# Residuals of three groups formed in PSUM by a unit product, and earlier loads in the last group

## The chip, the cores and the metric

One core of one Trainium2 chip runs the whole program in one launch. The metric is device time in microseconds, smaller is better. The engines are named as in the profile: PE (TensorE matmuls), PEld (its weight loads), DVE (VectorE), ACT (ScalarE), POOL (GpSimd) and SP (SyncE, which issues most DMAs here). PSUM is the memory that PE writes; SBUF is the other on-chip memory. Line numbers as L424 are those of the kernel before; those of the changed kernel are said to be so.

## The reference

Three stages in a row: a delta-rule attention with state, then two token-mixing blocks. The change lies in the attention.

```
q, k, v: (4, 8, 768, 48) fp32; beta: (4, 8, 768)
k_n = k / (norm(k) + 1e-06)
for t in range(768):                     # per batch and head, state is 48 x 48
    y[t]  = q[t] @ state
    v_old = state^T k_n[t]
    state = state + beta[t] * outer(k_n[t], v[t] - v_old)
x = y as (4, 768, 384)
h = gelu(x @ w_in); u, v = halves of h; v_n = layernorm(v) * g_ln
x = x + (u * (w_sg @ v_n + b_sg)) @ w_out
xk, xr = mixes of x with x one token earlier
out = sigmoid(xr @ w_r) * (relu(xk @ w_k)**2 @ w_v)
```

## The kernel before

**The attention** goes in 12 blocks s of 64 tokens. All 32 pairs of batch and head run side by side, in two halves o = 0 and 1 of 16 pairs. Two blocks make a group (6 groups, 0 to 5). Within a block the tokens depend on each other through a triangular matrix; the solver of a group (`solver`, on DVE) inverts its 32x32 diagonal parts into a tile DT, one group ahead of its use. A half block (s, o) goes through six stages:

- `st_rq`: 16 matmuls of k with the state into a PSUM tile rk (L444) and 16 of k with q into qk (L446); then the **residual**, and ACT's copies of qk (L453), which POOL masks (L454).
- `st_d0`: the first 32 tokens solved: 16 matmuls of DT with the residual, over rk (L432); ACT copies the result to u (L461).
- `st_l`: what they add to the other 32 tokens (L468), then the residual again.
- `st_d1`: the second 32 solved (L432), copied into the SQ tile by ACT (L479).
- `st_s` updates the state (L488, ACT's L494), `st_y` forms the output (L502, ACT's L507) and stores it.

The residual is the sum of the scaled v and what the matmuls left in rk: one DVE instruction that reads v from SBUF and rk from PSUM and writes the tile r to SBUF (`residual`, L424, 48 times). v is scaled by POOL (`scale_v`, L417) after its load (L247, two halves of a tile vk; L248 loads k beside it), some stages ahead of the block.

The two halves run three stages apart, one stage of one half after one of the other: (0,0) rq, d0, l, d1, (0,1) rq, (0,0) s, (0,1) d0 and so on. `run` goes through these 144 stages, counted by `point[0]`; a group is 24 of them. Between stages it fills PE's list with other work: `gram` (products of k for the solver two groups ahead), units of the next block (x @ w_in: L567, L618), and, where there is none, `keep_warm` matmuls on a zero tile (L659). `background` adds to DVE's list: layernorm steps, the solver, and **jobs**. A job rounds one tile of a weight into a high and a low part (`narrow`: load L148, six DVE steps L157 to L167, POOL L168 and L111, ACT L108), and for some weights stores the two parts back (L196).

What sets the order: PE, ACT, DVE and POOL run the attention in the order in which the program writes it (a manual schedule); each engine's queue is in order, so an instruction that waits holds up those behind it. SP's queue, and DVE, ACT and POOL after the attention, are ordered by the framework's scheduler.

When a job may start is set by three numbers: one runs at a time in the stages (`RUN[1]`), started at every fifth stage of a group, and its first step may come two stages after its load was issued (`LJ`):

```python
            if jobs and len(running) < RUN[1] and n % EVERY == 0:
                start_job()
```

**The mixing stage** (`mix`, `project`, L884, L139) and the **last stage** (L986 to L1008) follow; both are dense matmuls of PE on 384 columns, with DVE and ACT splitting their operands, and in the mixing stage the rest of the jobs.

Of the kernel before, what the change touches and what calls it, by code (L numbers as in the profile page):

```python
# [7 lines left out]
F32 = mybir.dt.float32  # L8
# [3 lines left out]
AF = mybir.ActivationFunctionType  # L12
ALU = mybir.AluOpType
# [3 lines left out]
B, H, S, D = 4, 8, 768, 48  # L17
# [3 lines left out]
P = 128  # L21
# [5 lines left out]
CW = 256  # L27
NPRE = 1.2
LJ = 2
LJ0 = 7  # L30
SV = 60
B0 = 1.4
PRE = 0.8
GRAM0 = 17
SOLVE0 = 3
RUN = (3, 1)
EVERY = 5
JLAG = 1
BUDGET = (1.2, 1.6, 1.2, 1.6, 1.6, 1.6)
UNITS = (4.64, 3.48, 2.32, 4.35, 3.19, 2.32)  # L40
# [34 lines left out]
def fused_kernel(  # L75
# [18 lines left out]
    V, A, G, T = nc.vector, nc.scalar, nc.gpsimd, nc.tensor  # L94
# [46 lines left out]

    def narrow(dram, i, j, hi, lo, cw=CW, pool=stg, lag=JLAG, parts=None):

        w = CW if pool is stg else cw
        raw = pool.tile([P, 2 * w], U32, name="raw", bufs=NRAW if pool is stg else 2)
        nc.sync.dma_start(out=raw[:, :2 * cw], in_=dram[i * P:(i + 1) * P, j:j + cw].bitcast(U32))  # L148
        w_lo = vw(raw, 0, [(2, cw)])
        w_hi = vw(raw, 1, [(2, cw)])  # L150
        yield 0
        a = pool.tile([P, w], U32, name="na", bufs=NNA if pool is stg else 2)[:, :cw]
        f = w_hi.bitcast(F32)
        af = a.bitcast(F32)
        t1 = cw / 1920 + 0.16
        t2 = cw / 960 + 0.16
        V.tensor_scalar(a, w_hi, 0x7FFFFFFF, None, op0=ALU.bitwise_and)  # L157
        yield t1
        V.tensor_scalar(af, af, E_LO_F, E_HI_F, op0=ALU.max, op1=ALU.min)
        yield t1  # L160
        V.tensor_scalar(a, a, 3, 0x3FFFFFFF, op0=ALU.logical_shift_left, op1=ALU.bitwise_and)
        yield t1
        V.scalar_tensor_tensor(a, w_hi, 0xC0000000, a, op0=ALU.bitwise_and, op1=ALU.bitwise_or)
        yield t2
        V.tensor_scalar(w_hi, a, 0xFF800000, None, op0=ALU.bitwise_and)
        yield t1
        V.scalar_tensor_tensor(f, w_lo, 2.0 ** -52, f, op0=ALU.mult, op1=ALU.mult)  # L167
        G.tensor_tensor(af, f, af, op=ALU.add)  # L168
        yield t2
        if hi is None:  # L170
            hi, lo = raw[:, :cw].bitcast(F32R), af.bitcast(F32R)
            parts.extend((hi, lo))
        yield lag, lambda: split(A, G, af, hi, lo)
# [11 lines left out]
    def scratch(dram, name, nblk, n, cw=CW, pool=stg):  # L185

        hi = dp.tile([nblk, P, n], F32, name=name + "_dh")
        lo = dp.tile([nblk, P, n], F32, name=name + "_dl")

        def job(i, j):  # L190
            parts = []
            yield from narrow(dram, i, j, None, None, cw, pool, parts=parts)

            def put():
                for d, x in zip((hi, lo), parts):
                    nc.sync.dma_start(out=d[i, :, j:j + cw], in_=x.bitcast(F32))  # L196

            yield 0, put

        return hi, lo, [lambda i=i, j=j: job(i, j) for i in range(nblk) for j in range(0, n, cw)]  # L200
# [12 lines left out]
    wo_dh, wo_dl, jobs = scratch(w_out, "wo", 4, DM, DM // 2)  # L213
# [6 lines left out]
    with ExitStack() as at:  # L220
        ap1 = at.enter_context(tc.tile_pool(name="ap1", bufs=1, side="right"))
# [12 lines left out]
        kT, kt, vt = {}, {}, {}  # L234
# [15 lines left out]
        def load_q(s, o):  # L250
            for h in range(2):
                r = 64 * (1 - h)
                nc.sync.dma_start(out=SQ[o][s % 2][h][r:r + D, :, D:], in_=q_d[s, o, h])

# [6 lines left out]
        def bank():  # L261
# [5 lines left out]
        load_k(1)  # L267
        Dm = ap1.tile([P, 32, 32], F32, name="Dm")
        V.memset(Dm, 0.0)
        SQ = [[[ap1.tile([P, 8, D + C], F32, name=f"SQ{o}{i}{h}") for h in range(2)]  # L270
               for i in range(2)] for o in range(2)]
        for i in range(2):
            for o in range(2):
                E = G if i else V
                E.memset(SQ[o][i][1][32:64], 0.0)
                E.memset(SQ[o][i][0][96:128], 0.0)
                for h in range(2):
                    r = 64 * (1 - h)
                    if i == 0:
                        E.memset(SQ[o][0][h][r:r + 64, :, 0:D], 0.0)  # L280
        G.memset(xT[:, :, :, 0:1], 0.0)
# [138 lines left out]
        RQs, ysts = {}, {}  # L420

        def residual(s, o):
            t = ap2.tile([P, 8, D], F32, name="r32")
            V.tensor_tensor(t, vt[s][:, 8 * o:8 * o + 8, :], RQs[o][:, :, 0:D], op=ALU.add)  # L424
            RQs[o, "r"] = t

        def solve(s, o, q):
# [8 lines left out]
        def st_rq(s, o):  # L436
            cur, k0 = SQ[o][s % 2], 8 * o
            R = RQs[o] = ps2.tile([P, 8, D], F32, name="rk")
            Q = ps2.tile([P, 8, C], F32, name="qk")
            for p in range(8):  # L440
                for h in range(2):
                    r, b0 = 64 * (1 - h), 64 * h
                    k = kT[s][r:r + 64, k0 + p, :]
                    T.matmul(R[r:r + 64, p, :], lhsT=k, rhs=cur[h][r:r + 64, p, 0:D],  # L444
                             start=(p == 0), stop=True, skip_group_check=True)
                    T.matmul(Q[b0:b0 + 64, p, :], lhsT=k, rhs=cur[h][r:r + 64, p, D:],  # L446
                             start=(p == 0), stop=True, skip_group_check=True)
            yield
            residual(s, o)
            for h in range(2):  # L450
                b0 = 64 * h
                pt = cur[h][b0:b0 + 64, :, D:]
                A.activation(pt, Q[b0:b0 + 64], AF.Copy, scale=-1.0)  # L453
                G.affine_select(out=pt, in_=pt, pattern=[[0, 8], [1, C]],  # L454
                                compare_op=ALU.is_gt, fill=0.0, base=0, channel_multiplier=-1)
# [18 lines left out]
        def st_d1(s, o):  # L474
            solve(s, o, 32)
            yield
            for h in range(2):
                r, b0 = 64 * (1 - h), 64 * h
                A.activation(SQ[o][s % 2][h][b0:b0 + 64, :, 0:D], RQs[o][r:r + 64], AF.Copy)  # L479

# [52 lines left out]
        later, vstat, streams, point = [], {}, [], [0, 0]  # L533
# [98 lines left out]
        def fill(n):  # L632
            n += owed[0]
            while n > 0 and (units or opened[0]):
                if not opened[0]:
                    done = min([i for i, _ in running] + [n_jobs - len(jobs)])
                    ready = [u for u in units if done >= (6, 12)[u[2]]]
                    if ready:
                        units.remove(ready[0])
                        opened[0] = ready[0][1]()  # L640
                    else:
                        break
                w, f = opened[0].pop(0)
                f()
                n -= w
            owed[0] = min(n, 0)
            if n > 0 and point[0] < 144:
                idle[0] += n
                keep_warm(int(idle[0]))
                idle[0] -= int(idle[0])  # L650
# [41 lines left out]
        running = []  # L692
        jobs = in_jobs + jobs
        n_jobs = len(jobs)

        def start_job(lead=LJ):
            j = jobs.pop(0)()
            running.append((n_jobs - len(jobs) - 1, j))
            next(j)
            streams.append([point[0] + lead, j, "job"])  # L700

        def early(n, t):
            for _ in range(n):
                background(t)
                while len(running) < 2 and len(jobs) > n_rest:
                    start_job(LJ0 if point[0] else LJ)
                point[0] += 1
# [14 lines left out]
        def whole(job):  # L722
            for _, f in job:
                f()

        stages = [st_rq, st_d0, st_l, st_d1, st_s, st_y]
        rest = [lambda j=j: whole(j) for j in diag[4:]]
        k = 0
# [27 lines left out]
        def run(fn, s, o):  # L756
            g, n = divmod(point[0], 24)
            point[1] = min(g, 1) + 1
            body = fn(s, o) if point[0] else iter(())
            next(body, None)  # L760
            gg, nn = divmod(point[0] - GRAM0, 24)
            if nn == 0 and 0 <= gg and gg + 2 < NG:
                grams.extend(gram(gg + 2))
            if n == 0 and g + 1 < NG:
                streams.append([point[0] + SOLVE0, solver(g + 1), "solve"])
            if jobs and len(running) < RUN[1] and n % EVERY == 0:
                start_job()
            if point[0]:
                background(BUDGET[stages.index(fn)] * (B0 if g == 0 else 1))
            while len(jobs) > n_rest and len(running) < RUN[0]:  # L770
                start_job()
            next(body, None)
            more = 0
            if grams and (point[0] - GRAM0) % GSTEP == 0:
                for _, f in grams.pop(0):
                    f()
                more = GU
            fill(more + UNITS[stages.index(fn)])
            point[0] += 1
# [9 lines left out]
        for i in range(3, 6):  # L789
            run(stages[i], 11, 1)  # L790
# [279 lines left out]
```

## Time and profile before

| | us |
|---|---|
| median of 3 runs | 815.54 (814.7 to 817.19) |
| the profiled execution: its own time | 811.44 |
| its span, first to last instruction | 809.7 |
| PE, DVE, ACT, POOL busy | 747.1, 583.3, 344.3, 186.9 |
| attention stages | about 50 to 375 |
| mixing stage | about 390 to 560 |
| last stage | about 560 to 810 |

One execution was profiled, on one core. A time of a timeline is in us from the span's start. An instruction's row has its duration, and in brackets how long its engine stood idle before it and what ended that wait. An arrow `r<-vk,rk` reads: r is written from vk and rk. PE issues every plain fp32 matmul as two records, so 16 of them are x32. The records of PE overlap, and their ends are modelled.

### The profile page before, as it was taken

Reading aid. Unit: us, or ns where it says so; the run is one execution under the profiler, and the core shown is the slowest. Engines: PE = TensorE matmul, PEld = TensorE weight load, DVE = VectorE, ACT = ScalarE, POOL = GpSimd, SP = SyncE. Lnnn points to the kernel's source line nnn. Section 1 sums busy time; section 2 is a strip of 40 time slices with the busy share of each in tenths; the row PEclk is TensorE's granted clock in tenths of the full one; section 3 lists DMA queues with packets and bytes.
Section 4 is the critical chain, followed back from the end, with each engine's and each line's share of the span. In section 5 each row is a group of like instructions: output and inputs, shape, how many; then the busy total and the mean of one; then the engine's idle time right before and its main releaser. Section 6 shows DMA issues by size and latency. Waiting matters only on the chain.

```text
span 809.7 us, 23901 instructions
## 1 busy us (share of the span) xinstructions
PE 747.1 (92%) x10206; PEld 656.5 (81%) x10206; DVE 583.3 (72%) x1253; ACT 344.3 (43%) x681; POOL 186.9 (23%) x197
## 2 busy tenths in 40 slices
PE   3368999999999998978989899899999999999998
PEld 3335667768778676767889799799999999999998
DVE  7989999689699698234779896988945655653442
ACT  2213454465555644634632231316744544542331
POOL 4125342232131323323324453340000000000000
PEclk9978999999999999989999889899999999999999
DMA  8403353354353443437987646449200000000000
GB/s 231 90 27 100 91 118 87 95 155 140 94 150 83 132 121 92 137 99 184 277 266 247 202 128 194 145 127 292 59 30 21 20 20 20 20 21 30 11 20 30
DMA packets 84970, 89.21 MB, mean 110 GB/s; under 512 B 25856, under 2 KB 68992, under 8 KB 84864
## 3 DMA queue, kind: packets, MB, share of 16 engines
q1 hardware_dynamic: 80128, 78.64, 32.8%
q0 software_dynamic: 4736, 9.04, 4.2%
q8 instruction: 80, 1.31, 0.7%
q14 instruction: 26, 0.21, 0.1%
HBM read 56.86 MB, written 26.08 MB: 102 GB/s over the span
## 4 chain that ended last, share of the span: by engine, by line
PE 60%; DVE 18%; DMA 7%; issue 6%; POOL 3%; ACT 2%; SPq 2%; DVEq 0%; POOLq 0%; ACTq 0%
PE ms L139 32%; PE ms L618 5%; PE ms L659 4%; PE rk L432 3%; PE ms L567 3%; PE ms L298 2%; DVE tmp L321 2%; PE ms L884 2%; DMA raw<-in_w_k_dram 2%; PE ms L502 2%; PE rk L468 2%; PE sps L488 2%; PE rk L444 2%; POOL na L168 1%; DVE na L157 1%
## 5 line engine op out<-in xcount | busy, mean ns | idle before, releaser
L168 POOL TENSOR_TENSOR na<-raw,na 128x256 f32<-128x256 f32 (+2 forms) x43 | 40.2, 938 | 149.7 <-DVE raw L167 110.0
L659 PE MATMUL ms<-warm 128*128 128x512 bf16 x222 | 62.1, 405 | 9.0 <-DVE warm L407 9.0
L139 PE MATMUL ms<-wvh,sh 128*128 128x384 f32 x192 | 64.9, 338 | 0.0
L139 PE MATMUL ms<-wvl,sh 128*128 128x384 f32 x192 | 64.9, 338 | 0.0
L139 PE MATMUL ms<-wvh,sl 128*128 128x384 f32 x192 | 64.8, 338 | 0.0
L139 PE MATMUL ms<-xm_hi,wkh 128*128 128x384 f32 x192 | 64.1, 334 | 0.0
L139 PE MATMUL ms<-xm_lo,wkh 128*128 128x384 f32 x192 | 64.1, 334 | 0.0
L139 PE MATMUL ms<-xm_hi,wkl 128*128 128x384 f32 x192 | 64.1, 334 | 0.0
L432 PEld LDWEIGHTS rk<-r,DT 32*32 32x32 f32 x1536 | 36.2, 107 | 28.7 <-DVE r L424 18.5
L111 DVE TENSOR_TENSOR sl<-r,sh 128x384 fp32r<-128x384 f32 x64 | 35.8, 559 | 30.3 <-ACT sh L108 30.3
L454 POOL TENSOR_SCALAR_AFFINE_SELECT SQ<-SQ 64x512 f32<-64x512 f32 x48 | 36.4, 759 | 86.6 <-ACT SQ L453 85.1
L432 PE MATMUL rk<-r,DT 32*32 32x48 f32 x1536 | 42.8, 205 | 13.0 <-DVE r L424 12.7
L424 DVE TENSOR_TENSOR r<-vk,rk 128x384 f32<-128x384 f32 x48 | 26.4, 549 | 38.4 <-PE rk L468 23.9
L108 ACT ACTIVATE sh<-r 128x384 fp32r<-128x384 f32 x64 | 33.6, 525 | 35.9 <-DVE r L990 35.9
L108 ACT ACTIVATE raw<-na 128x256 fp32r<-128x256 f32 (+2 forms) x31 | 13.7, 442 | 80.0 <-POOL na L168 78.1
L1006 DVE TENSOR_TENSOR ob<-th,ms 128x384 f32<-128x384 f32 x24 | 13.3, 553 | 43.3 <-PE ms L139 43.3
L300 PE MATMUL ms<-kT 64*32 64x64 f32 (+1 forms) x896 | 30.6, 225 | 13.9 <-issue 13.9
L618 PE MATMUL ms<-xh,wiu_hi 128*128 128x256 f32 x144 | 43.0, 298 | 0.0
L618 PE MATMUL ms<-xh,wiu_lo 128*128 128x256 f32 x144 | 42.9, 298 | 0.0
L618 PE MATMUL ms<-xl,wiu_hi 128*128 128x256 f32 x144 | 42.3, 294 | 0.6 <-issue 0.6
L990 DVE TENSOR_TENSOR r<-r 128x384 f32<-128x384 f32 x64 | 35.5, 554 | 9.6 <-ACT r L989 9.6
L157 DVE TENSOR_SCALAR na<-raw 128x256 uint32<-128x256 uint32 (+2 forms) x43 | 19.8, 461 | 30.1 <-DMA raw<-in_w_v_dram 7.7
(158 smaller groups left out, 2295.3 us busy)
## 6 DMA issues: line engine op xcount, KB each, us to landing
kT<-in_kt_d_dram SPq DMA_DIRECT2D x12, 512.0 KB, 4.5
u_d<-ug SPq DMA_DIRECT2D x48, 128.0 KB, 2.0
u<-u_d SPq DMA_DIRECT2D x8, 768.0 KB, 5.3
vn_d<-v SPq DMA_DIRECT2D x23, 256.0 KB, 3.9
vst<-vn_d SPq DMA_DIRECT2D x23, 256.0 KB, 3.4
SQ<-in_q_d_dram SPq DMA_DIRECT2D x48, 96.0 KB, 3.6
vk<-in_vk_dram SPq DMA_DIRECT2D x24, 192.0 KB, 3.9
vk<-in_vk_dram SPq DMA_DIRECT2D x12, 384.0 KB, 4.1
```

Source lines behind the costliest of these rows:

```text
L108: A.activation(hi, src, AF.Copy)
L111: eng_lo.tensor_tensor(lo, src, hi.bitcast(F32), op=ALU.subtract)
L139: T.matmul(pt, lhsT=a, rhs=b, start=(i == 0), stop=(i == n - 1))
L157: V.tensor_scalar(a, w_hi, 0x7FFFFFFF, None, op0=ALU.bitwise_and)
L168: G.tensor_tensor(af, f, af, op=ALU.add)
L300: T.matmul(gps[r + 32:r + 64, p, c0:c1], lhsT=t[r:r + 64, u, 32:64], rhs=vw2(t, r, 64, u * C + 32, [(0, (c1 - c0) // 32), (1, 32)]), start ...
L424: V.tensor_tensor(t, vt[s][:, 8 * o:8 * o + 8, :], RQs[o][:, :, 0:D], op=ALU.add)
L432: T.matmul(RQs[o][b0:b0 + 32, p, 0:D], lhsT=DT[b0:b0 + 32, u0 + p, :], rhs=t[b0:b0 + 32, p, :], start=True, stop=True, skip_group_check=True)
L454: G.affine_select(out=pt, in_=pt, pattern=[[0, 8], [1, C]], compare_op=ALU.is_gt, fill=0.0, base=0, channel_multiplier=-1)
L618: T.matmul(vstat["u"][:, 2 * P * d:2 * P * d + 2 * P], lhsT=w[:, c, ds_], rhs=a[:, c].rearrange("p b t -> p (b t)"), start=first, stop=last)
L659: T.matmul(o, lhsT=warm, rhs=vw(warm, 0, [(0, 4), (1, P)]), start=True, stop=True)
L990: V.tensor_tensor(r, r, r, op=ALU.mult)
```

## The change

In the groups 0, 4 and 5 (`SUMS`) the residual is no longer added by DVE. A unit matrix is built once on POOL. In `st_rq` of these groups PE first multiplies it with the scaled v, all 128 rows and 384 columns in fp32, into rk; the matmuls of k with the state then add onto it, so that rk holds the residual, and ACT copies it to r. In `st_l` the matmuls add onto it as before, and ACT copies again. For the very first half block the unit product comes after the matmuls. That is 12 products, 24 residuals off DVE and 24 copies onto ACT.

The second part: from stage 116 on (`LATE`, four stages ahead of the last group) two jobs may run at a time, one can be started at every fourth stage of the group, and a job's first step comes six stages after its load (`LJ5`).

```diff
--- before.py
+++ after.py
@@ -27,14 +27,17 @@
 CW = 256
 NPRE = 1.2
 LJ = 2
+LJ5 = 6
 LJ0 = 7
 SV = 60
 B0 = 1.4
 PRE = 0.8
 GRAM0 = 17
 SOLVE0 = 3
-RUN = (3, 1)
+RUN = (3, 1, 2)
+SUMS = (0, 4, 5)
 EVERY = 5
+LATE = 116
 JLAG = 1
 BUDGET = (1.2, 1.6, 1.2, 1.6, 1.6, 1.6)
 UNITS = (4.64, 3.48, 2.32, 4.35, 3.19, 2.32)
@@ -267,6 +270,10 @@
         load_k(1)
         Dm = ap1.tile([P, 32, 32], F32, name="Dm")
         V.memset(Dm, 0.0)
+        unit = ap1.tile([P, P], F32, name="unit")
+        G.memset(unit, 1.0)
+        G.affine_select(out=unit, in_=unit, pattern=[[-1, P]], compare_op=ALU.is_equal, fill=0.0,
+                        base=0, channel_multiplier=1)
         SQ = [[[ap1.tile([P, 8, D + C], F32, name=f"SQ{o}{i}{h}") for h in range(2)]
                for i in range(2)] for o in range(2)]
         for i in range(2):
@@ -421,7 +428,10 @@
 
         def residual(s, o):
             t = ap2.tile([P, 8, D], F32, name="r32")
-            V.tensor_tensor(t, vt[s][:, 8 * o:8 * o + 8, :], RQs[o][:, :, 0:D], op=ALU.add)
+            if s // 2 in SUMS:
+                A.activation(t, RQs[o], AF.Copy)
+            else:
+                V.tensor_tensor(t, vt[s][:, 8 * o:8 * o + 8, :], RQs[o], op=ALU.add)
             RQs[o, "r"] = t
 
         def solve(s, o, q):
@@ -437,15 +447,30 @@
             cur, k0 = SQ[o][s % 2], 8 * o
             R = RQs[o] = ps2.tile([P, 8, D], F32, name="rk")
             Q = ps2.tile([P, 8, C], F32, name="qk")
+
+            def values(start):
+                T.matmul(R[:].rearrange("p a b -> p (a b)"), lhsT=unit,
+                         rhs=vt[s][:, k0:k0 + 8, :].rearrange("p a b -> p (a b)"),
+                         start=start, stop=True, skip_group_check=True)
+
+
+
+            summed = s // 2 in SUMS
+            last = summed and (s, o) == (0, 0)
+            if summed and not last:
+                values(True)
             for p in range(8):
                 for h in range(2):
                     r, b0 = 64 * (1 - h), 64 * h
                     k = kT[s][r:r + 64, k0 + p, :]
                     T.matmul(R[r:r + 64, p, :], lhsT=k, rhs=cur[h][r:r + 64, p, 0:D],
-                             start=(p == 0), stop=True, skip_group_check=True)
+                             start=p == 0 and (last or not summed), stop=True,
+                             skip_group_check=True)
                     T.matmul(Q[b0:b0 + 64, p, :], lhsT=k, rhs=cur[h][r:r + 64, p, D:],
                              start=(p == 0), stop=True, skip_group_check=True)
             yield
+            if last:
+                values(False)
             residual(s, o)
             for h in range(2):
                 b0 = 64 * h
@@ -763,8 +788,9 @@
                 grams.extend(gram(gg + 2))
             if n == 0 and g + 1 < NG:
                 streams.append([point[0] + SOLVE0, solver(g + 1), "solve"])
-            if jobs and len(running) < RUN[1] and n % EVERY == 0:
-                start_job()
+            late = point[0] >= LATE
+            if jobs and len(running) < RUN[1 + late] and n % (4 if late else EVERY) == 0:
+                start_job(LJ5 if late else LJ)
             if point[0]:
                 background(BUDGET[stages.index(fn)] * (B0 if g == 0 else 1))
             while len(jobs) > n_rest and len(running) < RUN[0]:
```

PE's list gets the 12 products and is otherwise the same. Its rows at `st_rq` of (11,0), the last block's first half; ms are the units between the stages. Before:

```order
L567 MATMUL ms<-wiv_hi,xh 128x512
L567 MATMUL ms<-wiv_lo,xh 128x512
L468 MATMUL rk<-u_5907,GL 32x48 x16
L567 MATMUL ms<-wiv_hi,xl 128x512
L567 MATMUL ms<-wiv_hi,xh 128x512
L444 MATMUL rk<-SQ_111,kT_95 64x48
L446 MATMUL qk<-SQ_111,kT_95 64x64
```

And now (lines of the changed kernel: L452 the unit product, L466 and L469 the matmuls of k with state and q, L493 is `st_l`, L592 a unit):

```order
L592 MATMUL ms<-wiv_hi,xh 128x512
L592 MATMUL ms<-wiv_lo,xh 128x512
L493 MATMUL rk<-u_5922,GL 32x48 x16
L592 MATMUL ms<-wiv_hi,xl 128x512
L592 MATMUL ms<-wiv_hi,xh 128x512
L452 MATMUL rk<-vk,unit 128x384
L466 MATMUL rk<-SQ_114,kT_95 64x48
```

The product has come ahead of the matmuls of rq, behind the last unit.

ACT's list between (9,1)'s `st_l` and (10,0)'s `st_d0`, at the seam of groups 4 and 5: yst is an output, raw a job's rounding, SQ from qk and rk are the copies of `st_rq` and `st_d1`, ug a unit. Before:

```order
L507 ACTIVATE yst<-ms 128x8x64
L108 ACTIVATE raw<-na 128x192
L453 ACTIVATE SQ_109<-qk 64x8x64
L453 ACTIVATE SQ_110<-qk 64x8x64
L622 ACTIVATE ug<-ms 128x512
L479 ACTIVATE SQ_115<-rk 64x8x48
L479 ACTIVATE SQ_116<-rk 64x8x48
```

And now (L432 is the copy of the residual; L111 a job's rounding):

```order
L532 ACTIVATE yst<-ms 128x8x64
L111 ACTIVATE raw<-na 128x192
L432 ACTIVATE r_5573<-rk 128x384
L432 ACTIVATE r_5621<-rk 128x384
L478 ACTIVATE SQ_112<-qk 64x8x64
L478 ACTIVATE SQ_113<-qk 64x8x64
L647 ACTIVATE ug<-ms 128x512
L504 ACTIVATE SQ_118<-rk 64x8x48
L504 ACTIVATE SQ_119<-rk 64x8x48
```

The two copies, of (9,1)'s second residual and (10,0)'s first, stand right behind the job's rounding and ahead of the copies of qk.

SP's queue in the last group but one block: vk 64x768 is half of the v of block 11, vk 128x768 its k, xT the stores of an output into the next block's input. Before:

```order
L247 DMA vk<-in_vk_dram 64x768
L253 DMA SQ_115<-in_q_d_dram 48x8x64
L625 DMA u_d<-ug 128x2x128 x2
L607 DMA vn_d<-v 128x512
L196 DMA wo_dh<-raw 128x192
L196 DMA wo_dl<-na 128x192
L253 DMA SQ_116<-in_q_d_dram 48x8x64
L523 DMA xT<-yst 48x3x128 x4
L527 DMA xT<-yst 32x2x128
L527 DMA xT<-yst 16x2x128 x2
L527 DMA xT<-yst 32x2x128
L247 DMA vk<-in_vk_dram 64x768
```

And now (L250 v, L548 and L552 xT, L256 q):

```order
L250 DMA vk<-in_vk_dram 64x768 x2
L650 DMA u_d<-ug 128x2x128 x2
L632 DMA vn_d<-v 128x512
L199 DMA wo_dh<-raw 128x192
L199 DMA wo_dl<-na 128x192
L256 DMA SQ_118<-in_q_d_dram 48x8x64
L256 DMA SQ_119<-in_q_d_dram 48x8x64
L548 DMA xT<-yst 48x3x128 x4
```

Both halves of v now come together; one of them stood behind the eight stores of xT.

## Rows read from the trace of the kernel before

**Rows 1.** The page, part 1: busy us, share of the span, instructions.

```profile
PE 747.1 (92%) x10206; PEld 656.5 (81%) x10206; DVE 583.3 (72%) x1253; ACT 344.3 (43%) x681; POOL 186.9 (23%) x197
```

**Rows 2.** Who waited for whom, PE: us in all, times, longest us.

```profile
PE rk L432 <- DVE r L424: 12.7, 7, 4.3
PE ms L659 <- DVE warm L407: 9.0, 1, 9.0
PE ms L139 <- ACT gh L108: 6.0, 4, 2.5
```

**Rows 3.** PE's timeline: start us, us, instruction, count, idle before and its releaser.

```profile
57.50 0.87 PE L432 MATMUL rk<-r,DT 32*32 32x48 f32 x32 [2.06 <-DVE r L424]
...
73.89 0.87 PE L432 MATMUL rk<-r,DT 32*32 32x48 f32 x32 [2.15 <-DVE r L424]
...
75.65 1.49 PE L432 MATMUL rk<-r,DT 32*32 32x48 f32 x32
...
319.13 0.87 PE L432 MATMUL rk<-r,DT 32*32 32x48 f32 x32 [2.62 <-DVE r L424]
...
348.53 1.32 PE L432 MATMUL rk<-r,DT 32*32 32x48 f32 x32 [4.30 <-DVE r L424]
```

**Rows 4.** Windows: length, busy us and instructions of each engine, PEclk, DMA, GB/s.

```profile
core 0: us, PE busy (x) PEld busy (x) DVE busy (x) ACT busy (x) POOL busy (x), PEclk, DMA share, GB/s
57.00:63.00 6.00, 5.50 (x105) 3.32 (x105) 4.94 (x22) 2.47 (x5) 2.03 (x3) 0.72 0.17 48
75.00:84.00 9.00, 9.00 (x128) 5.26 (x128) 8.31 (x24) 2.96 (x7) 4.39 (x4) 0.62 0.32 91
347.00:356.00 9.00, 7.47 (x111) 6.75 (x111) 2.40 (x8) 1.72 (x4) 1.19 (x2) 0.62 0.33 101
455.00:475.00 20.00, 17.05 (x65) 13.85 (x64) 18.29 (x44) 4.53 (x11) 5.84 (x7) 0.74 0.57 176
505.00:520.00 15.00, 11.66 (x44) 8.92 (x43) 14.15 (x29) 4.41 (x9) 4.94 (x4) 0.77 0.44 155
660.00:810.00 150.00, 146.37 (x838) 146.04 (x836) 69.02 (x139) 56.80 (x124) 0.00 (x0) 1.00 0.06 21
57.00:105.00 48.00, 45.35 (x1073) 28.75 (x1073) 45.68 (x111) 18.35 (x39) 20.64 (x21) 0.89 0.30 87
```

**Rows 5.** DVE's timeline, the end of the solver and the last group.

```profile
102.69 1.97 DVE L412 STREAM_TRANSPOSE DT<-Dm 128x1024 f32<-128x1024 f32 x1
...
346.47 0.26 DVE L157 TENSOR_SCALAR na<-raw 128x192 uint32<-128x192 uint32 x1 [7.20 <-DMA raw<-in_w_out_dram]
...
347.93 0.55 DVE L424 TENSOR_TENSOR r<-vk,rk 128x384 f32<-128x384 f32 x1
```

**Rows 6.** Groups by line: shapes, count, busy us, mean ns, idle before and releasers.

```profile
L424 DVE TENSOR_TENSOR r<-vk,rk 128x384 f32<-128x384 f32 x48 | 26.4, 549 | 38.4 <-PE rk L468 23.9 <-PE qk L446 14.4
...
L461 ACT ACTIVATE u<-rk 128x384 f32<-128x384 f32 x24 | 11.8, 490 | 9.3 <-PE rk L432 7.9 <-ACT SQ L494 1.4
```

**Rows 7.** PE's timeline, the output of one half block.

```profile
66.43 1.15 PE L502 MATMUL ms<-SQ 128*64 128x64 f32 x32
```

**Rows 8.** ACT's timeline, two roundings ahead of stage work.

```profile
71.26 0.42 ACT L108 ACTIVATE wiu_hi<-na 128x256 fp32r<-128x256 f32 x1 [1.07 <-POOL na L168]
...
316.02 0.37 ACT L108 ACTIVATE raw<-na 128x192 fp32r<-128x192 f32 x1 [3.55 <-POOL na L168]
```

**Rows 9.** Timelines of POOL, PE and SP, block 11's v and its rq.

```profile
341.59 1.48 POOL L417 TENSOR_TENSOR vk<-vk,neT 128x768 f32<-128x768 f32 x1 [7.82 <-DMA vk<-in_vk_dram]
...
339.26 0.25 PE L444 MATMUL rk<-SQ,kT 64*64 64x48 f32 x1
...
323.99 0.53 SPq L247 DMA_DIRECT2D vk<-in_vk_dram  x1
```

**Rows 10.** DMA issues: count, KB each, median us to landing.

```profile
vk<-in_vk_dram SPq DMA_DIRECT2D x24, 192.0 KB, 3.9
```

## The prediction

> **What bounds the kernel now.** I read the page's busy shares first, then the list of who waited for whom on PE, then PE's timeline around those waits, then the windows with the granted clock, and last the queues of the engines that are waited for. The shares [rows 1] say that PE is the engine that carries the span: 92% busy, against 72% of DVE and 43% of ACT. But a share is an average over stages, and PE's own idle time is what can be won. The waits [rows 2] name it: the largest entry between two computing engines is L432, the two solves of a half block, behind the residual that DVE forms in L424: 12.7 us in 7 waits. (The 9.0 us behind warm lie at the start, ahead of the stages.)
>
> PE's timeline [rows 3] shows where they lie. Two are in group 0, at 57.50 (2.06 us) and 73.89 (2.15). Two are in the groups 4 and 5, at 319.13 (2.62) and 348.53 (4.30). What is left of the 12.7, another 1.6 us, is small pieces, which I count to the late groups. So groups 1 to 3 have nothing to win, and groups 0, 4 and 5 have 4.2 and 8.5 us. A wait also has a tail. The same form of work, 32 records of L432, takes 0.87 us at 73.89 and 1.49 at 75.65. The windows [rows 4] say why: the granted clock was 0.72 of full speed from 57 to 63, 0.62 from 75 to 84 and 0.62 from 347 to 356, each right behind a wait, so PE was at the lower of its two levels, 1.2 and 2.4 GHz, for part of each.
>
> Why the residual is late is seen on DVE [rows 5]. In group 0 DVE is full (45.68 of 48 us from 57 to 105 [rows 4]): it runs the solver of the next group and the roundings, and the residual takes its turn. At 346.47 it is another thing: DVE stood 7.20 us for the load of a raw weight tile, and the residual at 347.93, whose matmuls were long done, was queued behind that rounding.
>
> **The change, part by part.** 24 residuals of 549 ns leave DVE, 13.2 us, and 24 copies of the same tile come to ACT. The nearest row on ACT is u, a copy of the same 128x384 from PSUM, at 490 ns (both [rows 6]): 11.8 us. Neither sum is on the path; what counts is when the residual is ready. On ACT it starts when PE is done, unless something stands ahead of it in that queue (first rival).
>
> *The products.* 12 unit products are added to PE's list, and nothing else in PE's list changes. The trace holds no fp32 product of 128x384 with 128 rows, so I bound it. Every fp32 matmul leaves two records. Below: a 384-column record in the last stage takes 146.37/838 = 0.175 us [rows 4], two make 0.35. Above: y's fp32 matmuls (L502) are 32 records of 64 columns in 1.15 us [rows 7], in two column halves; if the halves ran side by side, 16 records one after another took 1.15, or 1.12 ns a column, and two records of 384 columns take 0.86 us. I take 0.65, a little nearer to L502, which is fp32 with 128 rows like the product. The Trainium skill, FP8 and Floating Point Precision, section TensorE Precision Notes, says that true FP32 takes four passes through the array; that speaks for the dear end, since with the last stage's 0.175 us for a pass it would be 0.70, and 7.7 us in place of the 7.2 below. The two records of each matmul do not tell two passes from four.
>
> The first product is free: it stands ahead of the warm matmuls, where PE waits 9.0 us in any case [rows 2]. The other 11 lie where PE is busy: 7.2 us, of it 2.0 in group 0 and 5.2 in groups 4 and 5 (at the bounds 3.9 and 9.5 in all). Each also waits for the scaled v of its block ahead of rq, where only DVE's add waited before (second rival).
>
> *Group 0.* Waits 4.2, clock 5.50 x 0.28 = 1.5 and 9.00 x 0.38 = 3.4, less 2.0 for products: 7.1 us. But I don't count all of that. The first solve of group 1 needs DT, whose transpose begins at 102.69 after DVE has been full throughout, so PE can gain little more than DVE does: the 7 residuals taken out ahead of it, 3.8 us. I take 4.0, with 0 and 7.1 as ends.
>
> *Groups 4 and 5.* Waits 8.5, clock 7.47 x 0.38 = 2.8, less 5.2: 6.1 us. That the last group's loads are issued ahead I cost at nothing by itself: with the residual off DVE, nobody of the stage waits for that rounding, whose cover is DVE's idle time there (2.40 of 9 us busy from 347 to 356). If the load were late again, a rounded tile would be late on ACT, with the copies behind it.
>
> *The rest.* The unit matrix (a memset and a select on POOL at the start) costs nothing: only memsets stand beside it then. In the mixing stage the lists of DVE, ACT and POOL come out in another order with the same jobs (23 roundings begun before it, as before). I take 0 for that, with the third rival as its bad end.
>
> **The sum.** 4.0 + 6.1 = 10.1 us off the profiled execution, 811.44 to 801.3. That execution lies 4.1 us below the median of the three runs shown, 815.54. Set against the median: **805.4 us**.
>
> **The rivals.**
>
> *Copies queue on ACT.* The copies of (9,1) and (10,0) come right behind a rounding in ACT's list (shown with the change). In the trace that rounding came at 316.02, after 3.55 us of waiting for POOL, which waits for DVE; and at 71.26 in group 0 one waited 1.07 [rows 8]. If that decides, PE waits as before, for ACT. Only the wait at 348.53 and its clock, 4.30 + 2.8 = 7.1, are gone, the products take 7.2, and the time is 815.6, no change. Against it: that DVE work also gets shorter by the residuals, and 316.02 is ahead of 319.13. 0.10.
>
> *The product waits for v.* Scaling the v of block 11 began at 341.59, after 7.82 us of waiting for its load, and rq of (11,0) began at 339.26 [rows 9]. With the product ahead of rq, PE would stand from there to 343.07, 3.8 us, with 2.8 of clock behind it: 805.4 + 6.6 = 812.0. So this part of the change would not do what it is there for. Against it: SP's list has now both halves of v together, where one went out at 323.99; with the 3.9 us that such a load takes to land [rows 10], v is there by 329. 0.08.
>
> *The mixing stage loses more.* This is the one that ends slower. Between 400 and 560, PE's projections wait for gh from ACT, which waits for DVE [rows 2]. From 455 to 475 such a wait cost 20 - 17.05 = 2.95 us and 17.05 x 0.26 = 4.4 of clock [rows 4]: 7.4 us; from 505 to 520 it was 3.3 + 2.7. DVE is full there (18.29 of 20), so a new order on it can move a gl or a w behind a rounding. With 1.4 more such waits the gain is gone; with two the time is 805.4 + 14.8 = 820.2. Against it: the work is the same, and it can as well lose one. 0.08.
>
> **How the numbers follow.** Forecast 0.74, rivals 0.10, 0.08, 0.08. About 0.3%, 2.4 us, is what a measurement of this kernel tells from no change. Faster: the forecast and most of the second rival, 0.80. The same: most of the first, and the third with one more wait, 0.10. Slower: the rest, 0.10. The range begins at 797 (group 0 at 7.1 and products at 0.35 give 799, and 2 for a lost wait in mixing) and ends at 814 (second rival with products at 0.86).
>
> **What would show it.** Right: no wait of L432 for a residual above 1 us in groups 0, 4 and 5; clock 1.0 from 340 on to the end of the stages; the unit product at 0.5 to 0.8 us of PE's time; the last solve some 10 us earlier, and the last stage as long as before. Wrong: waits of L432 for ACT's copy; a unit product that begins behind POOL's scaling; PE waiting for DT at the start of group 1 with the clock down; or the end of the stages 10 us earlier and the mixing stage as much longer.

## The result, and the profile after

| | before | changed |
|---|---|---|
| median, first comparison | 816.37 us (4 runs, 814.70 to 817.73) | 807.00 us (4 runs, 805.33 to 810.23) |
| ratio, with its 95% interval | | 0.9896 (0.9871 to 0.9922) |
| the profiled execution: time, span | 811.44, 809.7 | 810.23, 808.5 |

9.4 us faster, where 10.1 was forecast. But the profiled execution of the changed kernel was the slowest of its four, and that of before lay 4.9 us under its median, so this pair of traces differs by 1.2 us only. I had the changed kernel profiled once more (first experiment, "second execution" below) and read the three together. The line numbers are those of the changed kernel: L432 is the copy on ACT, L434 the residual on DVE, L442 the solve (L432 before), L452 the unit product, L493 st_l, L910 the first set of products of the mixing stage (L884 before), L111 and L114 the two halves of a split, L160 to L171 a rounding.

The page's busy shares of the changed kernel, against [rows 1]: PE is busy 7.1 us longer (part of that is a lower clock: in the second execution it is 748.8 us, 1.7 longer), DVE 14.0 less, ACT 8.3 longer.

```profile
span 808.5 us, 23944 instructions
...
PE 754.2 (93%) x10230; PEld 659.9 (82%) x10230; DVE 569.3 (70%) x1229; ACT 352.6 (44%) x705; POOL 186.7 (23%) x199
```

Who PE waited for from 45 to 300 us (first three lines) and from 300 to 375 (the others), against [rows 2]; the columns are the waiting line, the releaser, us in total, times, the longest:

```profile
PE rk L493 <- ACT u L486: 3.7, 2, 2.1
PE ms L527 <- ACT v L601: 1.4, 1, 1.4
PE ms L592 <- ACT ug L647: 0.2, 1, 0.2
...
PE ms L592 <- POOL xl L114: 1.0, 1, 1.0
PE ms L592 <- ACT xh L111: 0.9, 1, 0.9
PE ms L527 <- ACT ug L647: 0.5, 1, 0.5
PE ms L592 <- ACT ug L647: 0.4, 2, 0.2
PE rk L442 <- ACT r L432: 0.3, 1, 0.3
```

The 12.7 us behind the residual are gone; 0.3 us behind its copy is left. In group 0 the waits for u have grown from 1.3 to 3.7 us. The next table follows starts on PE's timeline through the program (us from the span's start; what is gained is against before). The halves are interleaved, so the last solve of group 0, (1,1)'s st_d1, stands right ahead of the first of group 1, (2,0)'s st_d0.

| | before | changed | changed, second execution |
|---|---|---|---|
| first solve | 50.86 | 50.25 | 51.41 |
| last solve of group 0 (block 1, half 1) | 105.26 | 104.83 | 102.65 |
| last solve ahead of block 8 (block 7, half 1) | 257.70 | 255.33 | 252.13 |
| last solve | 369.60 | 360.37 (9.2 gained) | 356.52 (13.1) |
| first L910 (L884 before) of the mixing stage | 396.0 | 392.1 (3.9) | 387.9 (8.1) |
| last L910 (L884 before) | 554.5 | 550.8 (3.7) | 544.8 (9.7) |
| end of the span | 809.7 | 808.5 (1.2) | 802.1 (7.6) |

So the stages gained about what was forecast (9.2) or more (13.1), and 5.0 to 5.3 us of it were lost again at once: from the last solve to the first mixing product it took 26.4 us before and 31.7 and 31.4 now. PE's timeline and ACT's in the changed kernel show where (times and durations in us, in brackets the idle time before and what ended it):

```profile
392.08 0.69 PE L910 MATMUL ms<-ws0h,vh 128*128 128x384 f32 x1 [4.32 <-ACT vh L111]
```

```profile
386.81 0.42 ACT L111 ACTIVATE raw<-na 128x256 fp32r<-128x256 f32 x1 [0.20 <-POOL na L171]
390.79 0.52 ACT L111 ACTIVATE ws0h<-wst 128x384 fp32r<-128x384 f32 x1 [3.57 <-DMA wst<-in_w_sg_dram]
391.40 0.63 ACT L111 ACTIVATE vh<-vst 128x512 fp32r<-128x512 f32 x1
```

The mixing stage needs vh, the high part of v. On ACT it is queued behind the sixth piece of w_sg, which waited for its load. SP issued that load at 387.63, behind three loads of v:

```profile
384.97 0.46 SPq L844 DMA_DIRECT2D vst<-vn_d  x1
385.48 0.94 SPq L650 DMA_DIRECT2D u_d<-ug  x2
386.46 1.07 SPq L844 DMA_DIRECT2D vst<-vn_d  x2
387.63 0.38 SPq L835 DMA_DIRECT2D wst<-in_w_sg_dram  x1
```

Before, vh stood ahead of that piece in ACT's list (vh at 393.85, the piece at 394.39), and PE did not wait. The granted clock came down with the wait: 0.50 from 388 to 394 in the second execution, 1.00 in that window before.

The last stage is 2.1 to 2.5 us longer (257.7 and 257.3 us from the last L910 to the end, 255.2 before). Most of that is lost near its start. PE by windows of 10 us in the changed kernel (busy us, instructions, clock):

```profile
570.00:580.00 10.00, 10.00 (x59) 1.00 0.01 3
580.00:590.00 10.00, 9.20 (x48) 1.00 0.05 20
590.00:600.00 10.00, 10.00 (x60) 1.00 0.11 41
```

48 records for the 58 of before in the same window, with waits for sh (0.5 us, ACT) and sl (0.3, DVE); the second execution has 49 from 570 to 580, with the same two waits.

### The profile page after: what moved, and what is told of

Same layout as the page of the kernel before. It is cut to its first block, busy times and chain, and to the rows that moved or that the text cites. A ratio compares the mean times of both kernels' runs of the same rounds, so it can differ in the third digit from the quotient of the medians.

```text
span 808.5 us, 23944 instructions
## 1 busy us (share of the span) xinstructions
PE 754.2 (93%) x10230; PEld 659.9 (82%) x10230; DVE 569.3 (70%) x1229; ACT 352.6 (44%) x705; POOL 186.7 (23%) x199
## 4 chain that ended last, share of the span: by engine, by line
PE 58%; DVE 17%; DMA 9%; issue 6%; ACT 4%; POOL 3%; SPq 2%; DVEq 0%; ACTq 0%; POOLq 0%
PE ms L142 27%; PE ms L592 5%; PE ms L643 4%; PE ms L684 4%; PE rk L442 3%; PE ms L305 3%; DMA vn_d<-v 2%; PE ms L527 2%; PE rk L493 2%; PE rk L466 2%; POOL na L171 2%; PE ms L910 2%; DVE gl L114 2%; PE sps L513 1%; DVE w L923 1%
## 5 line engine op out<-in xcount | busy, mean ns | idle before, releaser
L171 POOL TENSOR_TENSOR na<-raw,na 128x256 f32<-128x256 f32 (+2 forms) x43 | 40.0, 932 | 131.6 <-DVE raw L170 101.4
L114 DVE TENSOR_TENSOR sl<-r,sh 128x384 fp32r<-128x384 f32 x64 | 35.5, 555 | 30.2 <-ACT sh L111 30.2
L111 ACT ACTIVATE sh<-r 128x384 fp32r<-128x384 f32 x64 | 33.5, 524 | 35.7 <-DVE r L1016 35.7
L442 PEld LDWEIGHTS rk<-r,DT 32*32 32x32 f32 x1536 | 35.8, 106 | 16.2 <-issue 5.5
L611 DVE BATCH_NORM_STATS2 st<-v 128x6 f32<-128x512 f32 x24 | 16.5, 688 | 43.8 <-ACT v L601 43.8
L307 PE MATMUL ms<-kT 64*32 64x64 f32 (+1 forms) x896 | 32.5, 233 | 13.9 <-issue 13.7
L111 ACT ACTIVATE raw<-na 128x256 fp32r<-128x256 f32 (+2 forms) x31 | 13.6, 439 | 72.7 <-POOL na L171 72.7
L442 PE MATMUL rk<-r,DT 32*32 32x48 f32 x1536 | 42.3, 204 | 0.5 <-ACT r L432 0.3
L307 PEld LDWEIGHTS ms<-kT 64*32 64x32 f32 x896 | 28.5, 126 | 14.5 <-issue 14.5
```

What stands on the lines that cost most here:

```text
L111: A.activation(hi, src, AF.Copy)
L114: eng_lo.tensor_tensor(lo, src, hi.bitcast(F32), op=ALU.subtract)
L307: T.matmul(gps[r + 32:r + 64, p, c0:c1], lhsT=t[r:r + 64, u, 32:64], rhs=vw2(t, r, 64, u * C + 32, [(0, (c1 - c0) // 32), (1, 32)]), start ...
L442: T.matmul(RQs[o][b0:b0 + 32, p, 0:D], lhsT=DT[b0:b0 + 32, u0 + p, :], rhs=t[b0:b0 + 32, p, :], start=True, stop=True, skip_group_check=True)
```

## The experiments

"The changed kernel" is 804.73 us in the second comparison (ratio 0.9883) and 807.00 in the first (0.9896). Ratios are to runs of before on the same chip; across comparisons I compare ratios, and 0.001 is 0.8 us.

**The changed kernel once more.** No edit.

> The changed kernel as it is, to see how far its time and its trace differ between executions. 9.4 us below before, as in the first comparison (807.0 against 816.4). If the profiled execution of the first comparison (810.23) was the odd one, this profile shows a span near 805 and a higher granted clock from 10 to 65 us; if the gain is only 1 to 3 us, the first comparison was lucky.

804.73 us against 815.28, ratio 0.9883 (0.9848 to 0.9917): 10.5 us faster, span 802.1. The first profile was indeed a slow one, and the clock in group 0 tells for about half of it: 3.3 of the 6.4 us between the two spans. Windows of PE from 50 us, of the first execution:

```profile
50.00:53.00 3.00, 2.09 (x38) 1.00 0.06 10
53.00:56.00 3.00, 2.38 (x40) 0.65 0.50 171
56.00:59.00 3.00, 3.00 (x37) 0.50 0.00 0
59.00:62.00 3.00, 3.00 (x69) 0.71 0.26 87
```

And of the second:

```profile
50.00:53.00 3.00, 3.00 (x43) 1.00 0.06 19
53.00:56.00 3.00, 2.69 (x70) 1.00 0.47 161
56.00:59.00 3.00, 3.00 (x73) 1.00 0.02 5
59.00:62.00 3.00, 3.00 (x71) 1.00 0.53 166
```

The first st_l on PE, in the first execution and in the second:

```profile
53.62 1.26 PE L493 MATMUL rk<-u,GL 32*32 32x48 f32 x32 [1.53 <-ACT u L486]
...
53.51 0.87 PE L493 MATMUL rk<-u,GL 32*32 32x48 f32 x32 [0.26 <-ACT u L486]
```

In the first, st_l waited 1.53 us for u; the clock fell to 0.50, and the stretch from the first to the last solve of group 0 took 54.58 us. In the second the wait was 0.26, the clock stayed at 1.00 and the stretch took 51.24. Before took 54.40. Both st_l begin at nearly the same time: u stood on ACT behind two roundings that waited for POOL until 51.94 and 51.82, and PE had come 1.2 us earlier in the first.

**Without the earlier loads.**

```diff
-LATE = 116
+LATE = 999
```

> The products and copies in groups 0, 4 and 5 without the earlier loads. By the prediction the loads are worth nothing once the residual is off DVE: as the changed kernel, 9 to 10 us below before. Rival (the loads do the work in the last group): the late rounding now holds up ACT and the copies behind it, and the 4.30 us wait with its 2.8 us of clock, 7.1 in all, is back: 2 to 3 us below before.

807.37 us, 0.9913 (0.9879 to 0.9947): 7.9 below before. The rival's 2 to 3 us are excluded, so the products and copies carry most of the gain. Whether the loads add 2.6 us (807.37 to 804.73) the intervals do not settle; they overlap. In this trace DVE did stand 5.70 us for a late raw tile, as before the change, but PE did not wait behind it: its one wait for a copy in the late groups is 0.74 us and lies earlier. DVE and PE:

```profile
338.58 0.26 DVE L160 TENSOR_SCALAR na<-raw 128x192 uint32<-128x192 uint32 x1 [5.70 <-DMA raw<-in_w_out_dram]
...
323.34 0.87 PE L442 MATMUL rk<-r,DT 32*32 32x48 f32 x32 [0.74 <-ACT r L432]
```

**The earlier loads alone.**

```diff
-SUMS = (0, 4, 5)
+SUMS = ()
```

> The earlier loads alone, the residual stays on DVE in every group. By the prediction the wait at 348.53 goes (the rounding ahead of the residual on DVE no longer waits for its load): up to 7.1 us below before, as the two parts of the change would be substitutes in the last group, and group 0 and the wait at 319.13 are left. Rival (the loads only move the jobs, and with two jobs at a time DVE holds up other residuals): within 2.4 us of before.

810.05 us, 0.9945 (0.9922 to 0.9967): 5.2 below before. The wait at 348.53 is gone (PE busy 20.00 of 20 us from 340 to 360), but two residuals in group 0 still cost 4.1 us and four late ones 5.1. Waits of PE in this kernel, from 45 to 300 and from 300 to 375:

```profile
PE rk L442 <- DVE r L434: 4.1, 2, 2.1
...
PE rk L442 <- DVE r L434: 5.1, 4, 2.6
```

The two parts are in part substitutes for one wait: alone they gain 7.9 and 5.2 between medians, together 10.5, so 2.6 us are in both. The intervals alone do not settle that; the traces say the same of the late stages. From the last solve ahead of block 8 to the last solve the products alone take off 5.9 us, the loads alone 4.1, both 7.5.

**Without group 0.**

```diff
-SUMS = (0, 4, 5)
+SUMS = (4, 5)
```

> The change without its part in group 0 (products and copies in groups 4 and 5, earlier loads). By the prediction group 0 is worth 4.0 us: 5 to 6 us below before, some 4 us slower than the changed kernel. Rival (group 0 gives back on ACT and to the clock what it wins, as in the first two traces, where its last solve came only 0.4 us earlier): as the changed kernel, 9 us below before.

808.27 us, 0.9918 (0.9890 to 0.9946): 7.0 below before, 3.5 above the changed kernel on the same chip. Group 0 is worth 3.5, where 4.0 was forecast, though with overlapping intervals; between the traces it is 3.3 (spans of 805.4 and 802.1). The rival was read from the first execution, whose clock had fallen.

**Each product twice.**

```diff
             if summed and not last:
                 values(True)
+                values(True)
```

> Each of the 11 products ahead of the matmuls of k is issued twice (the second overwrites the first with the same values). By the prediction a product costs 0.65 us and all 11 lie on the path: 7.2 us slower than the changed kernel, some 2 us below before; by the spacing in the trace of the changed kernel (a product's first record to the next matmul's, 0.73 us) 8.0 slower. Rival (the list of PE in group 0 has slack behind ACT, so that part of the products is free there): 4 to 6 us slower than the changed kernel.

809.29 us, 0.9933 (0.9910 to 0.9955): 0.0037 to 0.0050 above the changed kernel, 3 to 4 us for 11 products between medians: the low end of the rival, or less, though the intervals leave anything from about 0 to 7. The trace says where they are cheap. In the stretch from the last solve ahead of block 8 to the last solve 8 more products take 109.31 us for 104.39, 0.6 each. From the first to the last solve of group 0 three take 52.08 for 51.24, 0.3 each: PE's waits for ACT from 45 to 300 us (for u, r and yst) are 3.7 us in place of 4.7, so part of a product fills time in which PE would stand. Of the 5.5 us by which the last solve comes later, the mixing stage's start shows 3.2 (391.1 for 387.9), but its last L910 5.5 again and the end 5.6 (807.7 for 802.1). So between these two traces the 11 products cost 5.6 us, 0.5 each; about 1 us of that is that the changed kernel's trace is the fastest of its four executions, 803.75 for a median of 804.73.

**All six groups.**

```diff
-SUMS = (0, 4, 5)
+SUMS = (0, 1, 2, 3, 4, 5)
```

> Products and copies in all six groups: 12 products more, 8.8 us at 0.73. By the prediction groups 1 to 3 have nothing to win (no wait for a residual), so 8 to 9 us slower than the changed kernel, within 2 us of before. Rival (DVE, busy for 80 to 85% there, begins solver and roundings earlier for 24 residuals less, 13 us, and this shows at the ends of those groups): no slower than 4 us above the changed kernel.

812.58 us, 0.9973 (0.9956 to 0.9989): 0.0077 to 0.0090 above the changed kernel, 6 to 7 us, a little under the 8 to 9. From the last solve of group 0 to the last one ahead of block 8, with 11 of the 12 products between them, it took 156.2 us for 149.5. With nothing to win, a product costs some 0.6 us, and DVE's 13 us bring nothing there.

**Loads ahead of the mixing stage in turn**, based on the changed kernel, as the last ones are.

```diff
-    ahead = [lambda i=i: load_ws(0, i) for i in range(6)]
-    ahead += [lambda c=c: load_v(0, c) for c in range(5)]
+    ahead = [f for i in range(5) for f in (lambda i=i: load_ws(0, i), lambda i=i: load_v(0, i))]
+    ahead += [lambda i=i: load_ws(0, i) for i in (5,)]
```

> Only the order of loads ahead of the mixing stage differs: each piece of w_sg is followed by a piece of v, where all six pieces of w_sg came first. My reading is that the gain of the stages is partly lost at the turn: in the changed kernel the first mixing matmul waits 4.3 us for vh, whose rounding stands on ACT behind the sixth piece of w_sg and its load. Then the wait goes and the mixing stage begins 3 to 5 us earlier than 387.9; if that is kept to the end the time is 3 to 5 us below the changed kernel. Rival (the same work is late in the mixing stage in any case, DVE being full there): the start is earlier and the end is not, within 2 us of the changed kernel.

802.74 us, 0.9845 (0.9822 to 0.9868), and in another comparison:

> The changed kernel with the loads ahead of the mixing stage in turn, once more, as the measure for the next two on the same chip: 12 us below before (ratio 0.985), as in its first run.

802.53 us, 0.9836 (0.9814 to 0.9857). That is 3 to 5 us below the changed kernel by the ratios (clear of the first comparison's interval, overlapping with the second's). The second trace has every solve within 0.3 us of the changed kernel's second execution (last solve 356.80 and 356.52), then 27.3 us to the first mixing product for 31.4, and ends 3.3 us earlier (798.8 for 802.1). ACT has vh early now, and the first product does not wait:

```profile
379.39 0.64 ACT L111 ACTIVATE vh<-vst 128x512 fp32r<-128x512 f32 x1 [1.56 <-DMA vst<-vn_d]
379.93 0.51 ACT L111 ACTIVATE ws0h<-wst 128x384 fp32r<-128x384 f32 x1
```

```profile
384.07 0.34 PE L910 MATMUL ms<-ws0h,vh 128*128 128x384 f32 x1
```

So the loss at the turn is shown to be that queue. Of the 3.9 us won at the first L910, 2.1 are left at the last and 3.2 at the end. The first trace of this kernel pairs with the first execution of the changed kernel (last solve at 360.30 and 360.37): 4.6 us won at the first L910, 7.7 at the end.

**ACT's rounding of w_in one stage later.**

```diff
-                                                lo[:, i, j - j0:j - j0 + CW], lag=0)
+                                                lo[:, i, j - j0:j - j0 + CW], lag=1)
```

> ACT's rounding of w_in comes one stage later in its list (lag 1 for 0), so that it is not issued while POOL's sum for it is still being formed. In the changed kernel ACT stood 2.5 and 4.1 us for POOL at such roundings in group 0, with a copy for PE behind them, and PE waited 2.9 us for u. If that queue is what group 0 still loses: those waits go, and the time is 2 to 4 us below the changed kernel. Rival (the copies are then late for another reason, or DVE's list bounds group 0): within 1.5 us of the changed kernel.

805.64 us, 0.9879 (0.9856 to 0.9903): no different from the changed kernel. What it removes is shown by ACT and PE in the changed kernel (second execution), a rounding that waits for POOL with u behind it, and st_l behind u:

```profile
76.99 0.42 ACT L111 ACTIVATE wiu_hi<-na 128x256 fp32r<-128x256 f32 x1 [4.07 <-POOL na L171]
77.32 0.47 ACT L486 ACTIVATE u<-rk 128x384 f32<-128x384 f32 x1
```

```profile
77.84 0.87 PE L493 MATMUL rk<-u,GL 32*32 32x48 f32 x32 [2.14 <-ACT u L486]
```

Those waits are gone, and the last solve of group 0 begins at 96.76, 5.9 us earlier than 102.65. Then group 1, whose residuals are on DVE, gives it back, with the clock at 0.73 from 105 to 115. PE in this kernel, the last solve of group 0 and the two of (2,0):

```profile
96.76 0.87 PE L442 MATMUL rk<-r,DT 32*32 32x48 f32 x32
100.62 0.87 PE L442 MATMUL rk<-r,DT 32*32 32x48 f32 x32 [1.80 <-DVE r L434]
110.15 1.49 PE L442 MATMUL rk<-r,DT 32*32 32x48 f32 x32 [3.13 <-DVE r L434]
```

DVE in this kernel: two roundings that stood ahead of DT now stand behind it, and the residual behind them and behind the next solver's first steps:

```profile
95.27 1.98 DVE L419 STREAM_TRANSPOSE DT<-Dm 128x1024 f32<-128x1024 f32 x1
97.07 0.30 DVE L160 TENSOR_SCALAR na<-raw 128x256 uint32<-128x256 uint32 x1
...
100.03 0.53 DVE L434 TENSOR_TENSOR r<-vk,rk 128x384 f32<-128x384 f32 x1
...
109.44 0.19 DVE L129 TENSOR_TENSOR rn_t<-rn_y 128x32 f32<-128x32 f32 x1
109.55 0.55 DVE L434 TENSOR_TENSOR r<-vk,rk 128x384 f32<-128x384 f32 x1
```

**Both, and then group 1 too.** Loads in turn and the later rounding:

> Loads in turn, and ACT's rounding of w_in one stage later. The first run of the later rounding ended group 0 5.9 us earlier and gave it back in group 1, whose residuals stand on DVE behind the next solver (waits of 1.80 and 3.13 us, the clock down behind them). If that holds: within 1.5 us of the kernel with the loads in turn alone, and the same two waits. Rival (the giving back was of one execution): 3 to 5 us below it.

801.45 us, 0.9828 (0.9807 to 0.9850), 1.1 below the loads in turn alone (802.53, same chip; the intervals overlap), with 3.4 us of waits for the residual of group 1. And with `SUMS = (0, 1, 4, 5)` besides:

> As the one before, and group 1 gets products and copies too: 4 products, 2.9 us at 0.73. If the residuals on DVE are what gives the 5.9 us back, the waits of 1.80 and 3.13 us for them go and 2 to 4 us are kept: some 2 us below the kernel with the loads in turn alone. Rival (group 1 is then late for the solver's tile DT, which DVE finishes no earlier): no gain, or the 2.9 us of the products slower.

**798.61 us, 0.9790 (0.9768 to 0.9811)**: 17.9 below before and 3.9 below the loads in turn alone, more than expected. The waits for DVE's residual are gone (one of 0.44 for ACT's copy is left); the second solve of block 2, at 110.97 in the changed kernel (second execution) and at 110.15 with the later rounding, begins at 106.09, and the last solve at 353.59, 2.9 earlier than 356.52. The four products are paid from what they free. This is the fastest kernel of the study.

## Why the prediction was right, step by step

**Total.** 10.1 us forecast, 9.4 and 10.5 measured. That is close in part by luck. At the last solve the two traces had gained 9.2 and 13.1 us, and the work behind it lost 8.0 and 5.5 of them, which the forecast put at 0. And the traces are set against an execution of before that lay 4 to 5 us under its median.

**The waits** of [rows 2, 3] for DVE's residual went, all of them, and in the late groups the low clock with them: PE was busy 19.76 of 20 us at 1.00 from 340 to 360, where a wait of 4.30 us and 0.62 of the clock stood before [rows 3, 4].

```profile
340.00:360.00 20.00, 19.76 (x408) 1.00 0.31 92
```

**A product.** Taken at 0.65 us, between 0.35 and 0.86; the trace has 0.74 from its first record to the next matmul's. This is PE's timeline at the upper level of the clock and, at 58.88, at the lower one, 1.41 us:

```profile
58.88 1.49 PE L452 MATMUL rk<-vk,unit 128*128 128x384 f32 x2
...
60.29 0.34 PE L466 MATMUL rk<-SQ,kT 64*64 64x48 f32 x1
```

```profile
351.34 0.81 PE L452 MATMUL rk<-vk,unit 128*128 128x384 f32 x2
352.08 0.25 PE L466 MATMUL rk<-SQ,kT 64*64 64x48 f32 x1
```

The Trainium skill, FP8 and Floating Point Precision, section TensorE Precision Notes, has four passes for true FP32; by that the estimate was 0.70, and the trace bears it out better than my 0.65.

That all 11 lie on the path in full is not borne out: doubling them cost 3 to 4 us between medians and 5.6 between two traces, not 7 to 8. In the late groups a further one costs 0.6 us, in group 0 0.3.

**Group 0.** 4.0 forecast, 3.5 measured between medians. The step that made 4.0 of 7.1 was the cap: the first solve of group 1 needs DT, so PE can gain little more than DVE does. The number came out, by another path than that. DVE and PE in the changed kernel (second execution):

```profile
100.08 1.98 DVE L419 STREAM_TRANSPOSE DT<-Dm 128x1024 f32<-128x1024 f32 x1
...
104.64 0.87 PE L442 MATMUL rk<-r,DT 32*32 32x48 f32 x32
```

DT is done at 102.06 and the first solve of group 1, (2,0)'s, begins 2.6 us later without a wait; before it was 104.66 and 107.24. No trace of this study has PE waiting for DT. What held PE back in group 0 was ACT's queue: u behind a rounding that waited for POOL, which took it up when DVE's last step of it was done (DVE from 74.58, POOL from 75.13, ACT from 76.99, u from 77.32; 2.9 us of waits for u in all). With that rounding one stage later the stretch from the first to the last solve of group 0 took 46.1 us, 8.3 less than before, so even the 7.1 of the sum without the cap was not all that could be had. DVE's list did hold PE then, by the residual of (2,0) at 100.62 and not by DT. I took the order of these lists as given, and two roundings could wait.

**Groups 4 and 5.** 6.1 forecast. From the last solve ahead of block 8 to the last solve the trace of before took 111.90 us, the changed kernel 105.04 and 104.39: 6.9 and 7.5. Without the loads it took 106.00, 5.9 less.

**The loads** were costed at nothing by themselves. With the residual off DVE they add 1.0 to 1.6 us in that stretch and perhaps 2.6 in the time (not settled). Alone they would have taken 5.2, which the forecast did not say: they cure the same wait from the other end.

**The rivals.** *Copies queue on ACT* was wrong for the late groups (0.3 us), whose wait it was to restore, and right for group 0 in a form that I had not put: mainly u behind a rounding, 3.7 us (2.9 in the second execution, with 0.6 for the residual's copy). *The product waits for v*: no wait of L452 for v. *The mixing stage loses more*: no more waits in it (158.5 us long before, 158.7 and 156.9 now), but its start lost 5 us, by just such a new order: a tile behind a load that it does not need. The steps that failed are "I take 0 for that" and, for its reason, the cap in group 0. The other loss behind the stages, 2 us near the start of the last stage, was not tried.

## What to carry to other kernels

A stage that ends earlier is worth only what the next can take: look at what its first instruction needs, and where that stands in the other engines' queues, before counting the gain. Where an add on a full engine holds up PE, let PE do it: a product of 0.74 us took the place of waits of 2 to 4 us, and it pays only in groups that wait. Two cures of one wait do not add up; cost each alone and both together.

## What the runs showed of the hardware

The same program came out in two ways. In one execution PE stood 1.53 us for u and the clock was 0.50 for some 6 us behind it, in the other it stood 0.26 us and the clock stayed at 1.00; from the first to the last solve of group 0 it took 54.58 and 51.24 us. The kernel with the loads in turn gave the same pair in its two traces: a wait of 1.69 us and 54.78, and one of 0.30 and 51.29. The length of a wait alone does not decide: 2.14 us at 77.84 in the second execution left the clock at 1.00.

The changed kernel's times range from 803.75 to 810.23 over both comparisons, and a single pair of profiles (1.2 us apart) would have hidden a gain of 10.
